# Other groups for 256 rows of w2 on the DMA engines, and their first quarter issued ahead of x

## Chip, cores and metric

The kernel runs on one core of a Trainium2 chip. The metric is the time of one execution on the device in microseconds (us). The span in a profile page is some 1.8 us shorter than that time. A run is labelled slow here when its time is over 1.5% above the fastest run of the same kernel, and fast otherwise.

## The reference, cut to what matters

Two tokens (B = 2, one position each) go through a normalisation, then through attention over the last 2048 positions of a cache, and beside it through a perceptron with a squared ReLU. All tensors are bf16.

```python
x = A_x                                   # [2, 1, 576]
xn = _layernorm(x)
return x + _A_ref(xn, A_k_cache, A_v_cache, A_wq, A_wo) + _B_ref(xn, B_w1, B_b1, B_w2, B_b2)

# _A_ref: 32 query heads, 16 heads of k and v, window W = 2048, head size 128
#   softmax(q k / sqrt(128)) v @ wo
# _B_ref:
h = jnp.einsum("bsd,df->bsf", x, w1) + b1          # F = 4608
h = jnp.where(h > 0, h, 0) ** 2                    # (shortened)
out = jnp.einsum("bsf,fd->bsd", h, w2) + b2        # w2 is [4608, 576]
```

Nearly all the time goes by while 53.6 MB of cache and weights are read. TensorE is busy for 70% of the span beside it, but the chain of work that ended last is 92% DMA (table below).

## The kernel before

Almost everything is loaded from the sync queue in large transfers over all 16 DMA engines. The last fourth of w2 has 1152 rows: 896 of them (FT = 7 rows for each of 128 partitions) come last of all on the sync queue, and 256 are taken out of that and loaded early from the scalar queue, in parts that only some of the engines carry. Every engine has the same bytes on the sync queue, so the grouping of these 256 rows decides, together with the instruction fetches, which engines end last.

`XS` holds the groups as (rows for a partition, partitions, engines): (3, 32, 8) is 96 rows on 32 partitions in four transfers of 8 partitions each, (8, 20, 5) is 160 rows on 20 partitions in four transfers of 5.

```python
    XS = ((3, 32, 8), (8, 20, 5))
    FT = (HW - sum(r * p for r, p, _ in XS)) // P      # 7
    # ... FX: first row of each group; CX: the columns of h that belong to the rows

    x_parts = [(s, i) for s, (_, xp, xe) in enumerate(XS) for i in range(xp // xe)]

    def issue_w2x():
        if x_parts:
            s, i = x_parts.pop(0)
            xr, xp, xe = XS[s]
            rows = B_w2[FX[s]:FX[s] + xr * xp, :].rearrange("(e i r) n -> i e (r n)", e=xe, r=xr)
            tc.keep_in_program_order(nc.scalar.dma_start(out=w2x_sb[s][i:xp:xp // xe, :], in_=rows[i]))

    xb_sb = const.tile([B + 1, D], BF16, name="xb_sb")
    x_sb = xb_sb[0:B, :]
    nc.scalar.dma_start(out=x_sb, in_=x2d)             # x: first on the scalar queue
    # ... sync queue: k of unit 0, wq; then the normalisation of x
```

The parts are issued one at a time, each after a load of k or v; the first after the load of v of unit 1. The matmuls that use them come late, when they have long landed.

```python
    def load_k(u):
        # ... sync queue
        if u >= 3:
            issue_w2x()

    def load_v(u):
        # ... sync queue
        if u >= 1:
            issue_w2x()

    def mlp_x():
        i = FT
        for w, (xr, xp, _) in zip(w2x_sb, XS):
            for r in range(xr):
                out_acc(mlp["h"][0:xp, N3 + i, :], lambda a, z: w[:, r * D + a:r * D + z])
                i += 1
```

## Time and profile before

| | before |
|---|---|
| time, median of 3 runs | 134.87 us (134.85 to 134.87) |
| span in the profile | 133.0 us |
| DMA share of the chain that ended last | 92% |
| rate of all 16 DMA engines in the middle | 430 GB/s |
| last weights land, on the span's clock | 129.66 us |

The table is read from the bottom: the last weights land at 129.66 us and only some 0.7 us of arithmetic follow. Between the start and that landing the DMA engines are full, so the time is made of bytes, of the rate at which they move, and of how evenly they are spread. The prediction shows the lines for this. First the rate in 40 equal slices of the span (GB/s, from the page): it stays near 430 from the second slice to the third from last.

```profile
GB/s 104 427 432 422 448 399 468 399 443 420 429 438 437 404 454 406 463 404 437 430 414 448 409 458 403 437 438 443 438 412 434 404 466 426 424 404 433 408 193 1
```

Then the start in order of time (start in us, duration, engine, line, what it does; ACTq is the scalar engine's sequencer, which issues the DMAs of the scalar queue):

```profile
0.72 0.56 ACTq L190 DMA_DIRECT2D xb_sb<-in_A_x_dram  x1
...
1.44 0.77 ACTq L186 DMA_DIRECT2D w2x_sb<-in_B_w_dram  x1
...
3.08 0.45 DVE L223 BATCH_NORM_STATS2 stats<-xb_sb 2x6 f32<-2x288 bf16 x1
...
6.62 0.51 PE L110 MATMUL pro_ps<-ident,tmp_x 2*128 2x2 bf16 x6 [6.62 <-DVE tmp_x L233]
```

The issue of x ends at 1.28 us, and its two packets start 0.4 us later, at 1.66 and 1.72. The first w2 part has been issued by 2.21, but its packets start at 5.70 to 5.94.

### The profile page before, as it was taken

The numbers are of one execution on the slowest core, as the hardware profiler recorded it, in microseconds if no ns is written. First come the engines' busy times: TensorE is split into PE (matmuls) and PEld (weight loads), VectorE is DVE, ScalarE is ACT, GpSimd is POOL, SyncE is SP. The second block draws the span as 40 slices with busy tenths as digits, with TensorE's granted clock in tenths as the row PEclk, the third lists the DMA queues.
The fourth block names the chain that finished last, engine by engine and source line by source line (L and its number), as shares of the span: only waits on it lengthen the run. The fifth ranks groups of instructions, "written<-read, shape, count | busy, mean of one in ns | idle before, by whom it ended". The sixth has DMA issues, their size and how long they took to land.

```text
span 133.0 us, 2082 instructions
## 1 busy us (share of the span) xinstructions
PE 93.0 (70%) x850; PEld 55.1 (41%) x850; DVE 58.8 (44%) x160; ACT 46.9 (35%) x65; POOL 5.4 (4%) x18
## 2 busy tenths in 40 slices
PE   0069646988597397767798597499785477829970
PEld 0059314465363243524554353437542144215640
DVE  6724405234575436457367684527430432070010
ACT  5715403177284263346385084343320400000010
POOL 7000000010100100010010100100010000000000
PEclk9999995559999959999999999657997775555698
DMA  3999999999999999999999999999999999999940
GB/s 104 427 432 422 448 399 468 399 443 420 429 438 437 404 454 406 463 404 437 430 414 448 409 458 403 437 438 443 438 412 434 404 466 426 424 404 433 408 193 1
DMA packets 4458, 53.74 MB, mean 404 GB/s; under 512 B 551, under 2 KB 682, under 8 KB 1230
## 3 DMA queue, kind: packets, MB, share of 16 engines
q1 hardware_dynamic: 4320, 53.32, 94.5%
q10 hardware_dynamic: 130, 0.31, 0.6%
q8 instruction: 6, 0.10, 0.3%
q14 instruction: 2, 0.02, 0.0%
HBM read 53.62 MB, written 0.00 MB: 403 GB/s over the span
## 4 chain that ended last, share of the span: by engine, by line
DMA 92%; PE 4%; SPq 1%; issue 0%; DVE 0%; DVEq 0%
DMA v<-in_A_v_cache_dram 43%; DMA k<-in_A_k_cache_dram 20%; DMA w<-in_B_w_dram 17%; DMA wq<-in_A_wq_dram 12%; PE kT_ps L110 2%; PE o_ps L107 1%; SPq L128 0%; SPq L135 0%; DVE fin_sb L594 0%; PE tail_ps L107 0%; DVEq L594 0%
## 5 line engine op out<-in xcount | busy, mean ns | idle before, releaser
L110 PE MATMUL kT_ps<-ident_f,k 128*128 128x128 f32 x256 | 42.8, 315 | 11.1 <-DMA k<-in_A_k_cache_dram 7.2
L110 PEld LDWEIGHTS kT_ps<-ident_f,k 128*128 128x128 f32 x256 | 33.3, 162 | 25.9 <-issue 11.4
L327 ACT COPY kT<-kT_ps 128x1024 bf16<-128x1024 bf16 x32 | 31.8, 1013 | 22.9 <-PE kT_ps L110 22.1
L329 DVE COPY kT<-kT_ps 128x1024 bf16<-128x1024 bf16 x32 | 21.9, 684 | 16.7 <-PE kT_ps L110 16.3
L107 PE MATMUL sc_ps<-kT,qz 128*32 128x512 bf16 x128 | 10.5, 413 | 5.8 <-DVE kT L329 5.8
L107 PE MATMUL o_ps<-v,pT 128*32 128x512 bf16 x128 | 12.1, 475 | 0.0
L359 ACT ACTIVATE p<-sc_ps,bias 128x512 bf16<-128x512 f32 x8 | 5.5, 687 | 17.9 <-DVE gown L355 17.9
L588 ACT COPY part<-out_ps 17x144 f32<-17x144 f32 x2 | 0.5, 268 | 23.8 <-DVE part L588 23.8
L348 DVE TENSOR_REDUCE m<-sc_ps 128x1 f32<-128x512 f32 x8 | 5.5, 692 | 7.2 <-PE sc_ps L107 7.2
L388 DVE SCALAR_TENSOR_TENSOR o<-o_ps,in_s,o 128x128 f32<-128x128 f32 x24 | 8.3, 346 | 0.5
L362 DVE STREAM_TRANSPOSE pT<-p 128x512 bf16<-128x512 bf16 x8 | 5.7, 710 | 6.4 <-ACT p L359 6.4
L386 DVE TENSOR_SCALAR o<-o_ps,in_s 128x128 f32<-128x128 f32 x8 | 2.7, 338 | 10.8 <-PE o_ps L107 10.8
L107 PE MATMUL out_ps<-wo,ws 128*17 128x288 bf16 x64 | 6.1, 364 | 1.6 <-DVE ws L421 1.6
L352 POOL PARTITION_ALL_REDUCE gmax<-m x8 | 2.9, 365 | 91.2 <-DVE m L350 91.2
L107 PEld LDWEIGHTS <-hT_sb 128*17 128x17 bf16 (+2 forms) x104 | 4.8, 105 | 4.0 <-issue 1.3
L107 PEld LDWEIGHTS <-qz 128*32 128x32 bf16 x128 | 2.2, 98 | 10.0 <-DVE kT L329 7.4
L107 PE MATMUL op_ps<-o,of_h 128*128 128x129 f32 x16 | 4.0, 339 | 3.3 <-DVE o L388 3.2
L107 PEld LDWEIGHTS <-xnT 128*2 128x2 bf16 x100 | 2.5, 94 | 8.6 <-issue 7.5
L107 PEld LDWEIGHTS <-ws 128*17 128x17 bf16 x64 | 3.5, 111 | 3.9 <-DVE ws L421 1.9
L110 PE MATMUL pro_ps<-ident,tmp_x 2*128 2x2 bf16 x6 | 0.5, 176 | 6.6 <-DVE tmp_x L233 6.6
L107 PEld LDWEIGHTS op_ps<-o,of_h 128*128 128x128 f32 x16 | 2.8, 221 | 5.3 <-DVE o L388 5.3
L107 PE MATMUL h_ps<-w,xnT 128*2 128x384 bf16 x48 | 3.2, 419 | 2.2 <-DMA w<-in_B_w_dram 2.2
(79 smaller groups left out, 58.5 us busy)
## 6 DMA issues: line engine op xcount, KB each, us to landing
k<-in_A_k_cache_dram SPq DMA_DIRECT2D x8, 2048.0 KB, 23.6
v<-in_A_v_cache_dram SPq DMA_DIRECT2D x8, 2048.0 KB
wo<-in_A_wo_dram SPq DMA_DIRECT2D x2, 2304.0 KB
w<-in_B_w_dram SPq DMA_DIRECT2D x2, 2304.0 KB
wq<-in_A_wq_dram SPq DMA_DIRECT2D x2, 2048.0 KB, 16.2
w<-in_B_w_dram SPq DMA_DIRECT2D x3, 1296.0 KB
w_rem<-in_B_w_dram SPq DMA_DIRECT2D x1, 576.0 KB, 35.2
w<-in_B_w_dram SPq DMA_DIRECT2D x1, 576.0 KB
```

What stands on the lines that cost most here:

```text
L107: tc.keep_in_program_order(nc.tensor.matmul(*a, **k))
L110: tc.keep_in_program_order(nc.tensor.transpose(*a, **k))
L327: nc.scalar.copy(out=kT, in_=kT_ps[:])
L329: nc.vector.tensor_copy(out=kT, in_=kT_ps[:])
L348: nc.vector.tensor_reduce(out=m1[:], in_=sc_ps[:], axis=AX.X, op=ALU.max)
L352: nc.gpsimd.partition_all_reduce(gmax[:], m2[:], channels=P, reduce_op=ReduceOp.max)
L359: nc.scalar.activation(out=p_sb[:], in_=sc_ps[:], func=ACT.Exp, bias=bias[:, 0:1], scale=scale, accum_out=o1[:, Dh:Dh + 1])
L362: nc.vector.transpose(out=pT[:].rearrange("p j r -> p (j r)"), in_=p_sb[:])
L386: nc.vector.tensor_scalar(scalar1=in_s[:, 0:1], scalar2=None, op0=ALU.mult, **kw)
L388: nc.vector.scalar_tensor_tensor(scalar=in_s[:, k:k + 1], in1=o1[:, 0:Dh], op0=ALU.mult, op1=ALU.add, **kw)
L588: cp(out=part[32 * i:32 * i + MB, :], in_=out_ps[32 * (i // 2):32 * (i // 2) + MB, (i % 2) * OQ:(i % 2 + 1) * OQ])
```

## The change

The intent: engines 0 to 4 end last because of their w2 rows, so 240 rows are spread over six engines (24 partitions of 10 rows, in four transfers of 6 partitions), and 16 over all engines (16 partitions of one row, one transfer). The first of the four transfers goes ahead of x, to lie in the stretch at the start in which the engines do nothing.

```diff
-    XS = ((3, 32, 8), (8, 20, 5))
+    XS = ((10, 24, 6), (1, 16, 16))
...
     xb_sb = const.tile([B + 1, D], BF16, name="xb_sb")
     x_sb = xb_sb[0:B, :]
+    issue_w2x()
     nc.scalar.dma_start(out=x_sb, in_=x2d)
```

## The prediction

> **What bounds the kernel now.** I read the page first (slices, queues, chain), then the busy time by stretches for the start and the end, then the chain of waits in order of time, and last the packet records and semaphore updates in the trace, which have a start, a duration, a size and a queue for each DMA packet.
>
> ```profile
> DMA  3999999999999999999999999999999999999940
> DMA packets 4458, 53.74 MB, mean 404 GB/s; under 512 B 551, under 2 KB 682, under 8 KB 1230
> q1 hardware_dynamic: 4320, 53.32, 94.5%
> q10 hardware_dynamic: 130, 0.31, 0.6%
> q8 instruction: 6, 0.10, 0.3%
> q14 instruction: 2, 0.02, 0.0%
> DMA 92%; PE 4%; SPq 1%; issue 0%; DVE 0%; DVEq 0%
> ```
>
> The transfers are busy from the first slice to the last but two and the chain that ended last is 92% DMA: what counts is when the last weights land. q1 is the sync queue (k, v and all weights), q10 the scalar queue (x, biases and the w2 rows of this change), q8 and q14 fetch instructions.
>
> Busy time by stretches, the last columns being granted clock, DMA share and GB/s:
>
> ```profile
> 0.00:1.60 1.60, 0.00 (x0) 0.00 (x0) 0.75 (x7) 0.28 (x1) 1.07 (x7) 1.00 0.00 0
> 1.60:2.10 0.50, 0.00 (x0) 0.00 (x0) 0.39 (x3) 0.50 (x1) 0.50 (x3) 1.00 0.02 5
> 60.00:120.00 60.00, 44.03 (x420) 24.88 (x418) 29.25 (x75) 19.46 (x27) 1.46 (x4) 0.82 1.01 430
> 126.60:127.20 0.60, 0.37 (x6) 0.14 (x3) 0.00 (x0) 0.00 (x0) 0.00 (x0) 1.00 0.84 338
> 127.20:128.10 0.90, 0.86 (x15) 0.72 (x16) 0.00 (x0) 0.00 (x0) 0.00 (x0) 1.00 0.69 270
> 128.10:128.70 0.60, 0.49 (x16) 0.18 (x14) 0.15 (x1) 0.00 (x0) 0.00 (x0) 1.00 0.42 154
> 128.70:129.40 0.70, 0.42 (x23) 0.27 (x25) 0.44 (x2) 0.14 (x1) 0.00 (x0) 1.00 0.10 36
> ```
>
> In the middle all 16 DMA engines are full (430 GB/s). At the end they stop one after another: between 126.6 and 129.4 us the idle shares weigh 0.6 x 0.16 + 0.9 x 0.31 + 0.6 x 0.58 + 0.7 x 0.90 = 1.35 us of every engine. The mean engine ends 1.35 us before the last one; so much an even load could give at most. At the start nothing moves for 1.6 us, and almost nothing until 2.1.
>
> The chain's last pieces (start, duration, what):
>
> ```profile
> 107.61 22.06 DMA w<-in_B_w_dram
> 129.66 0.04 issue
> 129.70 0.27 PE tail_ps L107 x4
> 129.97 0.03 DVEq L594
> 130.05 0.31 DVE fin_sb L594
> ```
>
> After the last w2 chunk lands (129.66) only 0.7 us of computing remain. TensorE waits for DMA little: in the timeline it idles 0.27 us at 127.24, about 0.1 at 128.6 and 0.28 at 129.32, with 0.04 before the last four matmuls. These 0.69 us are a second ceiling: were the weights earlier by more, TensorE would set the end.
>
> **Who is the last engine.** The packet records have no engine number, but on a full engine each packet starts where the one before ended (16384 B every 607 ns), and each engine runs the same 270 packets of q1 in the same order. That is enough to thread all packets into 16 tracks, and their scalar-queue packets tell which engines they are. When each track started its last semaphore packet (the landing follows 0.31 us later):
> - five tracks with 50.7 KB of w2 rows (engines 0 to 4): 128.59, 128.64, 128.64, and two that also carry a q14 instruction fetch, 129.17 and 129.35. These two have the 2304 B packet of the bias b1, so they are among engines 0 to 3;
> - three with 13.8 KB (engines 5 to 7): 127.26, and 128.63 and 128.68 with one q8 fetch each;
> - eight with none (8 to 15): four bare at 126.58 to 126.96, four with a q8 fetch at 128.13 to 128.20.
> A q8 fetch of 16 KB costs its engine 1.41 us (fetch and the stretched data packet after it take 2.02 us, less 0.607), the q14 fetches 0.76 and 0.58 us (129.35 and 129.17 less 128.59).
>
> **What the Trainium skill says.** "DMA: Bandwidth & Descriptors", Why a DMA increments its semaphore by 16 and not by 1: k is the largest number up to 16 that divides the slowest dimension of both sides, and on the hardware queues the lowest-numbered k engines are used, so 8, 5 and 6 rows go to engines 0-7, 0-4 and 0-5. The trace agrees for 8 and 5: eight tracks have the 3456 B packets and five of them the 9216 B ones. Same page, Queues, rings and completion order: each engine round-robins between rings packet by packet[...]; agrees, as q10 packets stand singly between q1 packets, and the last chunk's sixteen increments spread over 126.87 to 129.66 us. "Runtime: NRT & Kernel Launch", Instruction fetch mechanics: instructions come in 16 KiB blocks of 256; q8 shows six packets of 16384 B at 27.5, 49.1, 66.1, 83.4, 100.4 and 116.1 us, one per some 250 recorded TensorE instructions. TensorE's program is the same after the change, so I expect the same fetches. In order of time they hit two of engines 5 to 7, then four of 8 to 15; if they step up by one engine (inferred, not shown), that is 6 to 11, and engine 5 is the one without.
>
> **The change part by part.** Bytes and arithmetic stay: 256 rows before (3 x 32 + 8 x 20) and after (10 x 24 + 16), 11 stationary columns and 22 matmuls, the same FT = 7. The rows move.
> 1. Engines 0 to 4 lose four packets of 3456 and four of 9216 B. In the records each takes 131.5 and 343.5 ns to the next start, and its semaphore packet 5.5: 4 x 137 + 4 x 349 = 1944 ns.
> 2. Engines 0 to 5 get four packets of 11520 B. From 343.5 ns at 9216 and 385.5 at 10368: 427.5 + 5.5, times 4 = 1732 ns.
> 3. All 16 get one 1152 B packet: 47 + 5.5, some 53 ns.
> 4. Engines 6 and 7 lose 548 ns; engine 5 gains 1732 - 548.
> Sums: the worst two 129.35 and 129.17 - 1.944 + 1.732 + 0.053 = 129.20 and 129.01; the other three 128.43 to 128.48; engine 5 127.26 + 1.237 = 128.50; engines 6 and 7 128.14 and 128.18; the rest 0.05 later, at most 128.26. The worst gains 0.16 us by the regrouping alone.
> 5. The first quarter goes ahead of x. Today x, issued at 0.72 us, has its first packets at 1.66 and 1.72, and k's first packets start at 2.13 to 2.38. A 427 ns packet that starts at 1.7 on each of six engines lies in that empty stretch nearly whole; the later engines, some 60 ns apart like x's two, run into k's start by 0.1 or 0.2 us. But k's first packets take 0.88 to 1.39 us instead of 0.61 anyhow, so part of that may vanish too. I count 0.35 to 0.43 us off engines 0 to 5, 0.40 for the bounding ones.
> New last engine: 129.20 - 0.40 = 128.80, against 129.35: -0.55 us. That is under the 0.69 us that TensorE allows, so all of it reaches the end: 134.87 - 0.55 = 134.3; I put 134.35.
> What lies beside: x is issued some 0.7 us later and lands behind a large packet, perhaps at 3.5 us. The square root of the norm waits today for table loads until 5.63 us, which shift by the same 0.7; the first TensorE transposes of x go from 6.62 to 7.3 us and still end before k lands at 8.36. The scalar engine's instructions come in another order in the first three steps (the exponential stands after two copies instead of before). Loads are issued 20 us and more before they land, so such a shift doesn't starve the queue.
>
> **Rivals.** (a) The early packet is not hidden: k's packets start later on six engines. Then only 0.16 us is left, 134.7. For it: the two queues are issued at the same time and the sync issue already takes 0.63 us beside x's against 0.54 alone. Against it: the empty stretch.
> (b) A fetch lies on another engine than I think, or moves, as the scalar engine has fewer instructions. If engine 5 has a q8 fetch, it ends at 128.65 + 1.24 - 0.40 = 129.5 and the kernel is 0.15 us slower, 135.0. If a q14 fetch left engines 0 to 5, the worst were some 128.6 or 128.3; TensorE then caps the gain at 0.69, 134.2.
> (c) TensorE, at a granted clock of 0.55 between 120 and 126 us, ends the kernel by a slightly longer chain: the gain shrinks to some 0.3, 134.55.
> (d) The later x delays the query projection and so the first scores: with 20 us of queued loads it changes nothing at the end.
>
> **Range and chances.** From -0.16 (a) to -0.69 (ceiling), with room for a slower start and for (b): 133.95 to 134.85 holds eight in ten. All of it is far inside 2% (2.7 us): even an ideal load gives 1.35 us, 1%. Faster by over 2% 0.005, slower 0.01, within 0.985.
>
> **What would show it.** DMA share in the stretch before 2.1 us rising from nearly 0 to some 0.3; the last landing near 129.1 instead of 129.66 on the span's clock; the spread of the last sixteen increments shrinking from 2.8 to about 2.2 us; q8 still six packets and q14 two; TensorE's waits at the end nearly gone. Wrong if the landing moves by under 0.2 us (start not hidden), if the spread grows (fetch on engine 5), or if TensorE has no wait left while the end hasn't moved.

## The result, and the profile after

| | before | after |
|---|---|---|
| all runs of the same rounds, us | 134.85, 134.87, 134.87, 134.88 | 135.15, 134.79, 139.73, 140.47 |
| median | 134.87 | 137.44 |
| last weights land (profiled run, 135.15 us) | 129.66 | 130.02 |

The median of the changed kernel is 1.9% above that of the kernel before. Ratios in this document are the mean time of one kernel's fast runs over that of the other's fast runs of the same rounds, so they are not quite the ratio of the medians. Here the ratio is 1.0008, with a 95% interval from 0.9984 to 1.0032: it covers only the two fast runs of the changed kernel, on either side of the kernel before.

The two runs near 140 us carry the label slow. The kernel before ran 57 times, in turn with the other kernels and on the same chips, and was always between 134.76 and 135.09 us. Later profiles show the same loss in runs that are labelled fast, such as 136.97 us. So there are two questions: why is a good run not faster, and what makes a run bad?

**A good run.** The profiled run took 135.15 us. From its page, the scalar queue (q10, 0.31 MB as before) and the chain's shares; q8 and q14 again have six and two packets, the same lines as in the prediction:

```profile
q10 hardware_dynamic: 106, 0.31, 0.6%
...
DMA 85%; PE 10%; ACTq 1%; DVE 1%; issue 0%; DVEq 0%; ACT 0%
```

The start, in order of time, to be held against the same lines of before:

```profile
0.72 1.41 ACTq L186 DMA_DIRECT2D w2x_sb<-in_B_w_dram  x1
...
2.17 0.30 ACTq L191 DMA_DIRECT2D xb_sb<-in_A_x_dram  x1
...
7.74 0.81 DVE L224 BATCH_NORM_STATS2 stats<-xb_sb 2x6 f32<-2x288 bf16 x2 [3.19 <-DMA xb_sb<-in_A_x_dram]
...
9.80 0.51 PE L110 MATMUL pro_ps<-ident,tmp_x 2*128 2x2 bf16 x6 [9.80 <-DVE tmp_x L234]
```

The issue of the early part takes 1.41 us, so x is issued 1.45 us later than before (2.17 for 0.72) and lands at 7.71 us, not at 3.5; TensorE's transposes of x wait for it until 9.80. Nothing moved in the empty stretch (columns: stretch, us, then busy time and count of PE, PEld, DVE, ACT and POOL, granted clock, DMA share, GB/s; the other lines are the end of the kernel):

```profile
1.60:2.10 0.50, 0.00 (x0) 0.00 (x0) 0.40 (x3) 0.00 (x0) 0.50 (x3) 1.00 0.00 0
127.20:128.10 0.90, 0.51 (x10) 0.43 (x11) 0.00 (x0) 0.00 (x0) 0.00 (x0) 1.00 0.68 264
128.10:128.70 0.60, 0.60 (x14) 0.39 (x8) 0.00 (x0) 0.00 (x0) 0.00 (x0) 1.00 0.34 125
128.70:129.40 0.70, 0.59 (x20) 0.29 (x17) 0.49 (x2) 0.00 (x0) 0.00 (x0) 1.00 0.14 53
129.40:130.00 0.60, 0.30 (x8) 0.15 (x8) 0.11 (x1) 0.37 (x2) 0.00 (x0) 1.00 0.03 10
```

From 1.6 to 2.1 us the DMA share is 0.00, where I had predicted about 0.3. The packet records say when the early packets started: six of 11520 B at 5.00 to 5.05 us, in the midst of k. At the end the engines stop earlier than before in the mean (share 0.34 for 0.42 from 128.1 to 128.7 us), yet in the last line a share of 0.03 is left: less than one engine of 16 still works, and everything waits for it. Its landing closes the chain:

```profile
2.17 5.55 DMA xb_sb<-in_A_x_dram
...
107.94 22.08 DMA w<-in_B_w_dram
130.02 0.04 issue
130.07 0.26 PE tail_ps L107 x4
...
130.41 0.31 DVE fin_sb L595
```

The landing is 0.36 us later than before (130.02 for 129.66). Threading the packet records into one track for each engine, as in the prediction, gives the starts of the last semaphore packets:

| track | before | after |
|---|---|---|
| two of engines 0 to 3, with a q14 fetch | 129.17, 129.35 | 129.05, 129.23 |
| engines 0 to 3, without | 128.59, 128.64 | 128.27, 128.40 |
| engine 4 | 128.64 | 128.21 |
| engine 5 | 127.26 to 128.68 (one of the three of 5 to 7) | **129.67**, with a q8 fetch at 27.7 us |
| 6 and 7 | the other two of those | bare 126.37 to 127.04, |
| 8 to 15 | bare 126.58 to 126.96, with a fetch to 128.20 | with a fetch to 128.34 |

The last engine is one that was never last before. It has the large w2 packets but not the packet of b1, so it is engine 4 or 5; the experiments tell why I call it 5.

**A bad run** was not profiled in this round, so no trace shows the runs of 139.73 and 140.47 us themselves. The first experiment, the same kernel again, caught one.

### The profile page after: what moved, and what is told of

It reads as the page before. It is cut to its first block, busy times and chain, and to the rows that moved or that the text cites. A ratio compares the mean times of both kernels' runs of the same rounds, so it can differ in the third digit from the quotient of the medians.

```text
span 133.4 us, 2081 instructions
## 1 busy us (share of the span) xinstructions
PE 88.6 (66%) x850; PEld 52.0 (39%) x850; DVE 58.4 (44%) x160; ACT 46.6 (35%) x65; POOL 5.4 (4%) x18
## 4 chain that ended last, share of the span: by engine, by line
DMA 85%; PE 10%; ACTq 1%; DVE 1%; issue 0%; DVEq 0%; ACT 0%
DMA k<-in_A_k_cache_dram 32%; DMA v<-in_A_v_cache_dram 28%; DMA w<-in_B_w_dram 17%; PE kT_ps L110 7%; DMA w2x_sb<-in_B_w_dram 4%; DMA xb_sb<-in_A_x_dram 4%; PE o_ps L107 3%; ACTq L186 1%; PE sc_ps L107 1%; DVE stats L224 1%; DVE fin_sb L595 0%; PE tail_ps L107 0%; PE op_ps L107 0%; DVE mv L226 0%; DVEq L595 0%
## 5 line engine op out<-in xcount | busy, mean ns | idle before, releaser
L110 PE MATMUL kT_ps<-ident_f,k 128*128 128x128 f32 x256 | 40.4, 304 | 11.4 <-DMA k<-in_A_k_cache_dram 8.6
L110 PEld LDWEIGHTS kT_ps<-ident_f,k 128*128 128x128 f32 x256 | 31.2, 155 | 26.2 <-issue 14.5
L107 PE MATMUL sc_ps<-kT,qz 128*32 128x512 bf16 x128 | 9.7, 383 | 6.4 <-DVE kT L330 5.0
L107 PE MATMUL o_ps<-v,pT 128*32 128x512 bf16 x128 | 13.3, 519 | 0.0
L107 PE MATMUL out_ps<-wo,ws 128*17 128x288 bf16 x64 | 5.6, 341 | 1.6 <-DVE ws L422 1.6
```

Source lines behind the costliest of these rows:

```text
L107: tc.keep_in_program_order(nc.tensor.matmul(*a, **k))
L110: tc.keep_in_program_order(nc.tensor.transpose(*a, **k))
```

## The experiments

Sixteen kernels ran, in five groups (1 to 4, 5 to 8, 9 to 12, 13 to 15, and 16), on chips 7, 4, 7, 11 and 13; kernels of one group share their runs of the kernel before. Differences within a group are the safest, as the chip is the same. The theories: the runs near 140 us are a slow state of the chip or the launch and not of the kernel (called A where an expectation has letters); the late x delays what follows (B). Later there was a third: engines 0 to 5 lag behind the others and that stops something (S). Each fell, as told below.

### 1. The changed kernel again

No edit. It ran to see whether long runs come back on another occasion, and to catch one in a profile.

> The changed kernel once more, to see how often it falls to the long time and, with luck, to get a trace of it. Theory A (the long runs are a fault of the chip that day): all runs 134.8 to 135.2. Theory B (the long runs belong to the kernel: x now stands behind a large scalar-queue packet, and how long the pair waits behind k on the DMA engines differs from run to run): again two groups, near 135.0 and near 140, with a third to two thirds of the runs long.

Measured: 139.98, 136.44, 138.52, 139.40, 135.20, 136.78 us, beside eleven runs of the kernel before at 134.79 to 134.99. The run of 139.98 us is the profiled one. Its rate in 40 slices:

```profile
GB/s 147 405 436 420 426 439 432 413 441 425 432 424 383 379 360 370 370 360 375 356 379 368 436 427 427 446 426 427 427 427 434 425 436 426 428 419 426 412 166 1
```

Ten slices in the middle move 356 to 383 GB/s, all others but the ends about 430. By stretches (columns as above), ahead of it, in it and after it:

```profile
30.00:40.00 10.00, 5.12 (x36) 3.06 (x34) 3.79 (x8) 3.58 (x6) 0.37 (x1) 0.68 1.02 434
42.00:73.00 31.00, 24.24 (x195) 14.15 (x194) 15.65 (x38) 13.61 (x18) 1.09 (x3) 0.83 1.01 368
76.00:86.00 10.00, 6.37 (x51) 3.36 (x50) 5.37 (x14) 3.54 (x6) 0.37 (x1) 0.83 1.01 433
```

The DMA share is 1.01 in all three: the engines have work without a pause, and each packet takes longer. In the records a 16384 B packet takes 611 ns outside and about 720 inside, on all 16 engines alike. The good run of the changed kernel has no such stretch:

```profile
42.00:73.00 31.00, 25.07 (x227) 15.33 (x226) 18.61 (x45) 15.07 (x19) 1.09 (x3) 0.94 1.01 429
```

nor has the kernel before:

```profile
42.00:73.00 31.00, 23.15 (x201) 13.25 (x201) 17.56 (x43) 14.63 (x19) 1.09 (x3) 0.94 1.01 430
```

The size fits. In 31 us at 368 GB/s there is 31 x (1 - 368/430) = 4.5 us of lost transfer, and this run is 4.8 us above the good one (139.98 less 135.20). The stretch runs from about 41.4 to 74 us. At 41.1 to 41.9 us the records show the packets of the 16-row transfer, one for each engine. The kernel before sends nothing like it from the scalar queue. That made it the first suspect.

### 2. The new groups alone, x first

```diff
-    XS = ((3, 32, 8), (8, 20, 5))
+    XS = ((10, 24, 6), (1, 16, 16))
```

> The new groups (10 rows on 24 partitions, 1 on 16) with x issued first as before. Theory B: x lands near 2 us again, no long runs at all, all runs within 0.3 us of each other. Theory F (an instruction fetch of 16 KB lies on engine 5, which now carries 47 KB): the last track ends near 129.6 to 129.9 and the time is 134.9 to 135.4, slower than before by 0.1 to 0.5. If the prediction's reading was right (engine 5 free of fetches): 134.7.

Measured: 136.97, 136.22, 135.94, 136.76, 135.25, 136.71 us, all labelled fast, ratio 1.0106 [1.0074, 1.0139]. So the long runs come without the early issue: theory B falls as their cause. The trace of the 136.97 us run has a stretch from 53 to 64.6 us:

```profile
42.00:52.00 10.00, 8.31 (x84) 4.98 (x82) 5.75 (x14) 5.50 (x7) 0.36 (x1) 1.00 1.01 431
54.00:64.00 10.00, 7.47 (x75) 4.35 (x75) 5.84 (x14) 4.72 (x6) 0.37 (x1) 1.00 1.01 362
```

Here the 16-row packets lie at 51.7 to 53.1 us, as the kernel issues them one load of k or v later. The stretch has moved with them. The loss, some 11 us x (1 - 362/431) = 1.8 us, is most of the 2.1 us by which the run lies above the kernel before; the rest is the lagging engine.

### 3. The early issue alone, old groups

```diff
+    issue_w2x()
     nc.scalar.dma_start(out=x_sb, in_=x2d)
```

> The old groups with the first part (3 rows each on engines 0 to 7) issued ahead of x. Theory B: long runs near 140 appear here too, though nothing of the grouping changed; in short runs x lands 4 us later than before and the end is where it was, 134.7 to 135.0. If the long runs come from the grouping: none here.

Measured: 134.82, 134.76, 134.80, 134.82, 134.75 us, ratio 0.9993 [0.9982, 1.0005]. No run is long. In the trace the start is as in the changed kernel:

```profile
0.72 1.38 ACTq L186 DMA_DIRECT2D w2x_sb<-in_B_w_dram  x1
```

The issue takes 1.38 us, the early packets (3456 B here) start at 4.79 to 5.13 us and x's at 6.20 and 6.47. So x lands as late as in the changed kernel and costs nothing at the end: rival (d) of the prediction is right. The run can't tell whether the early packet is worth its full 0.13 us on eight engines, because the interval holds both that and nothing; the packet times say that it isn't hidden.

### 4. Two parts ahead of x

The changed kernel with `issue_w2x()` twice ahead of the load of x.

> The changed kernel with two quarters ahead of x instead of one. Theory B: x lands later still (over 9 us in the good case) and the long runs get more frequent or the only ones, 138 to 142; that would also give a trace of the long state. Theory A: 134.8 to 135.4.

Measured: 135.16, 135.38, 135.31, 135.74 us, ratio 1.0044 [1.0030, 1.0059]. The packets of the second part start at 6.57 to 6.75 us, right after the first's, and x's at 8.34 and 8.48. Doubling the early bytes hides nothing more and only delays x by another 1.7 us. The profiled run (135.16 us) has no slow stretch, though its 16-row transfer went at 31.5 to 33.2 us: that transfer doesn't always bring one. Nor did it in the good run of the result, where it went at 41.4 to 42.1 us.

### 5. The 16 rows on eight engines

```diff
-    XS = ((3, 32, 8), (8, 20, 5))
+    XS = ((10, 24, 6), (1, 16, 8))
```

With x first. The 16 rows now go in two transfers of 8.

> New groups of ten rows with x first, but the last 16 rows in two transfers on engines 0 to 7 instead of one on all 16. In the two long traces all 16 engines slow from 611 to 720 or 733 ns per 16 KB packet at once, 1 us after the 16-engine transfer, and stay slow for 12 to 33 us. Theory R (the transfer of one row on each of 16 engines sets this off): no slow stretch here, 134.7 to 135.3 by the fetch on engine 5. Theory S (the lag of engines 0 to 5 against the others sets it off): slow stretches remain, 135.3 to 140.

Measured: 135.06, 136.71, 135.47, 135.13, 135.10, 135.70 us, ratio 1.0049 [1.0018, 1.0081]. Far fewer long runs, but 136.71 is one, and only the 135.06 us run was traced. It is clean, and its last engine starts its last semaphore packet at 129.67 us, as in the changed kernel. What lengthened 136.71 stays open.

### 6. The 16-row transfer first of the parts

The kernel of experiment 2 with the last part moved to the front.

```diff
+    x_parts = x_parts[-1:] + x_parts[:-1]
```

> New groups with x first and the 16-engine transfer as the first w2 part, the four ten-row parts after it. Theory R: the slow stretch begins right after that transfer, near 7 us, or, if it needs more than that transfer, does not occur at all. Theory S: it begins after the last ten-row part, near 50 us, as in the trace with the old order, 135.3 to 140.

Measured: 136.30, 135.36, 135.28, 137.05, 136.87, 135.60 us, ratio 1.0090 [1.0051, 1.0129]. In the trace (136.30 us) the 16 packets go at 5.0 to 5.5 us and the stretch lies from 6 to 17:

```profile
6.00:17.00 11.00, 8.11 (x54) 6.51 (x55) 4.24 (x10) 4.05 (x4) 0.00 (x0) 1.00 1.02 395
20.00:30.00 10.00, 8.82 (x62) 4.75 (x55) 3.60 (x10) 2.60 (x6) 0.36 (x1) 0.55 1.01 432
```

At 5 us no engine has had a w2 row yet, so engines 0 to 5 cannot lag: theory S falls. Three kernels have now put the transfer at three times, and the stretch began within about 1 us of it each time.

### 7. The kernel before with one 16-row transfer added

All else is as before; after the last w2 part a dummy transfer of 16 rows of w2 goes to a tile that nothing reads.

```diff
-    const.tile([P, 96], F32, name="pad_0")
+    junk = const.tile([16, D], BF16, name="junk")
+    junk_done = []
...
+        elif not junk_done:
+            junk_done.append(1)
+            tc.keep_in_program_order(nc.scalar.dma_start(out=junk[:], in_=B_w2[FX[0]:FX[0] + 16, :]))
```

> The kernel before with one more transfer after its last w2 part: 16 rows of w2 into a scratch tile, one on each of the 16 engines, 53 ns each. Theory R: slow stretches start near 65 us, after this transfer, and runs spread over 135 to 138. Theory S: none, 134.9 to 135.0.

Measured: 139.93, 134.88, 143.45, 137.19, 140.84, 135.02 us. The two good runs equal the kernel before (ratio of fast runs 1.0006 [0.9989, 1.0024]); the others lose up to 8.6 us. In the trace of 139.93 us the 16 packets go at 71.0 to 71.7 us and the stretch lasts from 73 to 121 (ahead of it, its first part and its last):

```profile
60.00:70.00 10.00, 7.50 (x73) 4.44 (x70) 4.62 (x11) 5.19 (x7) 0.36 (x1) 1.00 1.01 429
74.00:84.00 10.00, 7.13 (x71) 4.22 (x67) 5.84 (x15) 4.72 (x6) 0.36 (x1) 1.00 1.02 391
...
114.00:121.00 7.00, 5.36 (x40) 2.30 (x40) 1.42 (x5) 0.00 (x0) 0.00 (x0) 0.50 1.00 384
```

This settles theory A: a kernel that was never long in 57 runs becomes long in four of six by 18 KB that nobody uses. The slow stretch belongs to that transfer.

### 8. 96 rows on all engines in place of 16

A layout that should do the balancing better: 160 rows on five engines as before, 96 rows over all 16.

```diff
-    XS = ((3, 32, 8), (8, 20, 5))
+    XS = ((8, 20, 5), (1, 96, 96))
```

> 160 rows in four parts of 8 rows on engines 0 to 4 and 96 rows in one transfer of six rows on every engine; engine 5 gets no more than its share. From the tracks of the kernel before: the worst engine ends at 129.35 - 1.94 + 1.40 + 0.29 = 129.10, so 134.6 if no slow stretch comes. Theory R: slow stretches after the transfer on 16 engines, 135 to 138. Theory S: none, since engines 0 to 4 lag less than before.

Measured: 135.78, 135.82, 136.04, 135.74, 135.85 us, ratio 1.0074 [1.0061, 1.0087]; a miss by 1.2 us, and steady. The transfer's packets, six for each engine, start from 50.2 to 54.6 us, and the trace is slow meanwhile: 395 GB/s from 50 to 54 us, with 16 KB packets up to 10% longer. That is 4 x (1 - 395/430) = 0.3 us, too little for 1.2 us, and where the rest goes I did not find out.

### 9. The added transfer, spread over the partitions

Experiment 7 with the destination on every eighth partition, 0 to 120.

```diff
+            tc.keep_in_program_order(nc.scalar.dma_start(out=junk[0:P:8, :], in_=B_w2[FX[0]:FX[0] + 16, :]))
```

> The kernel before with the same extra 16-row transfer, but its rows written to partitions 0, 8, 16 and so on to 120 instead of 0 to 15. Theory D (sixteen engines meet while they write into the same few partitions): no slow stretch, all runs 134.9 to 135.0. Theory Q (it is that all 16 engines turn aside to a second queue at nearly the same time): slow stretches as with partitions 0 to 15, some of the six runs at 137 to 143.

Measured: 134.94, 135.01, 135.02, 134.97, 135.22 us, ratio 1.0013 [1.0001, 1.0025]. No run is long, and the trace is clean where that of experiment 7 was slow:

```profile
74.00:84.00 10.00, 8.78 (x61) 5.53 (x58) 4.98 (x12) 3.92 (x6) 0.37 (x1) 0.66 1.01 431
```

### 10. The added transfer, its rows from far apart

Experiment 7 with the destination as there (partitions 0 to 15) and 16 rows spread over the whole of w2.

```diff
+            tc.keep_in_program_order(nc.scalar.dma_start(out=junk[:], in_=B_w2[0:F:F // 16, :]))
```

> The same, written to partitions 0 to 15, but its rows read from all over w2 (every 288th row) instead of 18 KB in a row. Theory M (sixteen engines meet on one short piece of memory): no slow stretch, all 134.9 to 135.0. Theories D and Q: some runs at 137 to 143.

Measured: 136.71, 134.95, 136.90, 142.92, 143.48, 135.04 us. As bad as experiment 7; the trace of 136.71 us has the stretch from 74 us on, with the transfer at 72.7 to 73.5:

```profile
74.00:85.00 11.00, 7.74 (x76) 4.34 (x75) 7.44 (x18) 4.74 (x7) 0.36 (x1) 1.00 1.01 375
```

It is the side that is written that matters, not where the rows are read. Experiment 9 ran in the same rounds on the same chip, so the two compare without a change of chip.

### 11. Eight rows added in place of 16

```diff
+            tc.keep_in_program_order(nc.scalar.dma_start(out=junk[0:8, :], in_=B_w2[FX[0]:FX[0] + 8, :]))
```

> The same with 8 rows on engines 0 to 7 instead of 16 on all. Theory Q: no or rare slow stretches, as the kernel before has four such transfers and never ran long in 40 runs. If some runs are long: it is the lateness of the transfer, not its sixteen engines.

Measured: 135.08, 135.05, 134.99, 134.96, 134.98 us, ratio 1.0010 [0.9997, 1.0023]; no long run, and the trace is clean. The scratch tile stands in place of a padding tile, so the tiles behind it may lie elsewhere; here and in 12 this is as in 7 and 10, so it is not what makes runs long.

### 12. The added transfer on the sync queue

Experiment 7 with `nc.sync` in place of `nc.scalar`.

> The same 16 rows issued on the sync queue between two tiles of the caches, so that no engine has to turn to another queue. Theory Q: none slow, 134.9 to 135.0. Theories D and M: some runs at 137 to 143.

Measured: 135.03, 134.93, 134.93, 134.89, 134.89 us, ratio 1.0005 [0.9993, 1.0017]; no long run, and the trace is clean:

```profile
74.00:84.00 10.00, 7.16 (x74) 4.22 (x67) 6.35 (x16) 4.62 (x6) 0.36 (x1) 1.00 1.02 436
```

The same 16 rows to the same partitions do no harm in the queue that carries all the rest. One thing changed along with the queue: the sixteen packets now start over 2.9 us (76.88 to 79.78), where in the five traces with a long stretch they started within 0.5 to 1.4 us. So the queue and the packets' coming together are not told apart. Coming together is not enough by itself: in experiment 9 they came within 0.8 us.

### 13. The changed kernel, its 16 rows on the sync queue

```diff
-            tc.keep_in_program_order(nc.scalar.dma_start(out=w2x_sb[s][i:xp:xp // xe, :], in_=rows[i]))
+            queue = nc.sync if xe > 8 else nc.scalar
+            tc.keep_in_program_order(queue.dma_start(out=w2x_sb[s][i:xp:xp // xe, :], in_=rows[i]))
```

> The changed kernel with its last part, 16 rows on 16 engines, issued on the sync queue; all else the same. If that transfer on the scalar queue is the cause of the long runs: none over 135.6, and two values, near 134.8 and near 135.2, by whether an instruction fetch falls on engine 5. If not: again a third to two thirds of the runs at 136 to 140.

Measured: 135.20, 135.24, 135.35, 135.31, 134.81, 135.12 us, ratio 1.0019 [1.0007, 1.0031]. The long runs are gone, and the stretch that was slow in experiment 1 is full:

```profile
42.00:73.00 31.00, 25.61 (x226) 15.41 (x226) 18.81 (x45) 14.97 (x19) 1.10 (x3) 0.93 1.01 430
```

What is left is the good run's loss: the trace again has one lagging engine, whose last semaphore packet starts at 129.72 us.

### 14. The new groups, x first, the 16 rows on the sync queue

The kernel of experiment 2 with the same queue line.

> The new groups with x first as before and the 16 rows on the sync queue. If the transfer is the cause: 134.7 to 135.3, no slow stretch, where the same kernel with the scalar queue gave 135.25 to 136.97. Against the kernel above it shows what the early issue is worth: by the tracks nothing, within 0.1 us.

Measured: 135.23, 135.09, 134.72, 134.69, 135.01, 134.87 us, ratio 1.0002 [0.9991, 1.0014]. No run is long. The traced one is the 135.23 us run, with its lagging engine at 129.77 us. The runs lie between two ends, 134.7 and 135.2. The median is 134.94 for 135.22 in experiment 13, more than the 0.1 us that was expected; six runs of each, with both ends in both, can't say whether that is the early issue or how often a fetch falls on the lagging engine. Neither kernel had a long partner on this chip: that the queue is the cure rests on 12 beside 10 for one chip, and on 13 and 14 across chips.

### 15. Two short-row transfers over all engines, on the sync queue

A further try at a better balance; the copies after the transposes of h are written as a loop over the groups.

```diff
-    XS = ((3, 32, 8), (8, 20, 5))
+    XS = ((4, 20, 5), (1, 80, 80), (1, 96, 96))
...
+            queue = nc.sync if xe > 8 else nc.scalar
```

> A balance that avoids both faults: x first, 80 rows in four parts of 4 on engines 0 to 4, and 176 rows as 80 and 96 partitions, 5 and 6 rows on every engine, on the sync queue; six stationary columns instead of eleven. From the tracks of the kernel before: the worst engine 129.35 - 1.94 + 0.72 + 0.53 = 128.66, one of 8 to 15 with a fetch 128.20 + 0.53 = 128.73; so 0.62 us less than before, 134.2. If small packets or a slow stretch eat it: 134.9 and more.

Measured: 136.32, 136.27, 136.30, 136.39 us, ratio 1.0105 [1.0092, 1.0118]: a miss by 2.1 us. The short rows go at about 58 and 63.7 us, and there the rate falls:

```profile
58.00:64.00 6.00, 5.22 (x47) 3.09 (x49) 3.10 (x7) 3.04 (x3) 0.00 (x0) 0.90 1.02 388
```

That window holds 6 x (1 - 388/430) = 0.6 us of the 2.1; the rest was not traced to a cause.

### 16. 96 rows on 32 partitions over all engines, on the sync queue

```diff
-    XS = ((3, 32, 8), (8, 20, 5))
+    XS = ((8, 20, 5), (3, 32, 32))
...
+            queue = nc.sync if xe > 8 else nc.scalar
```

> 160 rows in four parts of 8 on engines 0 to 4 as in the kernel before, and the other 96 as 3 rows on each of 32 partitions, two packets of 3456 bytes per engine, in one transfer on the sync queue; x first. From the tracks of the kernel before: the worst engine 129.35 - 1.94 + 1.40 + 0.27 = 129.08, those with a fetch at most 128.5, so 0.27 us less than before whatever engine a fetch falls on: 134.6, all runs within 0.2 us. If the short packets on all engines set off a slow stretch here too: 135 to 137.

Measured: 135.38, 135.11, 135.24, 135.31, 135.45 us, ratio 1.0034 [1.0020, 1.0047]; a miss by 0.7 us, with a short slow stretch as well:

```profile
57.00:61.00 4.00, 3.09 (x33) 1.91 (x25) 2.80 (x8) 3.14 (x5) 0.20 (x1) 1.00 1.03 376
```

Its cost is some 4 x (1 - 376/430) = 0.5 us. The two last experiments bound the finding of 12 to 14: the sync queue is free of the long stretch for the 16-row transfer, but larger transfers of short rows over all engines cost more there than their bytes. No kernel beats both of the two compared.

### What the runs say together

| runs | count | over 135.6 us |
|---|---|---|
| kernel before | 57 | 0 |
| 16 rows to partitions 0 to 15, from the scalar queue, over 16 engines (the changed kernel, 1, 2, 4, 6, 7, 10) | 38 | 24 |
| no such transfer, or spread, or of 8 rows, or on the sync queue (3, 5, 9, 11 to 14) | 38 | 2 (both of 5) |

Experiments 8, 15 and 16, with larger transfers of short rows, are not in the table: they are slower in every run, and their losses are explained only in part.

The long stretch was traced only where three properties met: 16 engines (7 and 10 against 11), the destination in partitions 0 to 15 (7 and 10 against 9), and the scalar queue (7 and 10 against 12). On one chip, in the same rounds, 10 was long in four of six runs and 9, 11 and 12 in none of fifteen. The untraced 136.71 us of experiment 5, without such a transfer, stays an exception, and with the queue the spacing of the packets changed too (12). What happens in the chip is not shown. The Trainium skill, "DMA: Bandwidth & Descriptors", section Back-pressure in remote DMA, says that a saturated port on the written side holds up the engines behind it and their other queues. It says so of transfers between cores; that the destination decides here (9 against 10) would fit such a cause within one core, but no run shows a port. Why the state lasts for 11 to 48 us after packets of 50 ns, and why it ends, is open. In several traces it ends near an instruction fetch (74.1 us in experiment 1, 121.1 in 7, 64.6 in 2); I saw this and did not test it. It is no rule: the fetches at 51.2 us in experiment 1 and at 84.4 and 102.7 in 7 ended nothing, and in experiment 6 the stretch ended near 17.6 us with no fetch there.

**Which engine lags.** Of the fifteen traces that I threaded, seven are of kernels with the old groups: there engines 0 to 4 never had a q8 fetch, and engines 5 to 7 had two or none. In all eight traces with the new groups exactly one of engines 4 and 5 had one. The one that can have a fetch in the old groups is engine 5, so I take it to be that; the records don't number engines, so this is inferred. Which of the six fetches hits it changes from launch to launch, even for the same kernel: the first (at 27.7 us) in the profiled run of the result, the third (74.1 us) in experiment 1. All eight traced runs with the new groups had such a fetch, and clean ones among them took 135.06 to 135.23 us. The runs at 134.7 to 134.8 us (134.79 of the result, 134.72 and 134.69 of 14) fit launches without one on engine 5; none of them was traced.

## Why the prediction was wrong

The prediction was 134.35 us, within 133.95 to 134.85; the median is 137.44, and of the first four runs only 134.79 lies in the range. That it stays within 2% by the median (1.9%) is luck: half of the first four runs are over 3.5% longer.

**Steps 1 to 3, the sums for engines 0 to 3: right.** Without the hidden part the prediction put the two tracks with a q14 fetch at 129.20 and 129.01 us; they are at 129.23 and 129.05. So the worth of a packet by its size holds within 0.04 us, and the gain of 0.16 us by regrouping was there on these engines (0.12 measured). The other engines of this class are at 128.21 to 128.40, for 128.43 to 128.48.

**Step 3, "some 53 ns" for the 16-row transfer: the failed step behind the median.** The packets do take 51 ns. The step counted their bytes and nothing beyond. What they set off costs 1.8 us in experiment 2, 4.5 in experiment 1 (this kernel), and 8.6 by time in the worst run of 7. Neither the profile of before nor any rival had a sign of it: before has no transfer of this kind.

**Step 4, engine 5 "is the one without" a fetch: failed.** I took the order of the fetches over the engines for a rule that goes on ("if they step up by one engine"), from a single trace. The placement changes from launch to launch. Rival (b), engine 5 with a fetch, is what happened in the good runs. Its size was nearly right: without the hidden 0.40 it puts engine 5 at 129.9 us, and the track is at 129.67, which is 1.46 us after engine 4's 128.21. Its 135.0 us is close to the 135.15 of the profiled run.

**Step 5, 0.40 us hidden at the start: failed, it was 0.** I read the empty stretch from 0 to 2.1 us as room for any transfer issued first. x's two packets did use it, but a part over six engines was issued in 1.41 us, beside the issues of the sync queue, and its packets started only at 5.0, behind k. The hint was in the trace of before: its first w2 part was issued by 2.21 us and its packets came at 5.7. Going first moved them to 5.0, from 5.54 in experiment 2, and not to 1.7. Rival (a) had this.

**Rivals (c) and (d).** TensorE did not set the end: it waits 0.89 us at 127.59 and 0.30 at 129.70 in the good run. x was to be issued 0.7 us later and was issued 1.45 later, as the early part took 1.41 us to issue; it landed 4 us later than I thought and still costs nothing (experiment 3). "Loads are issued 20 us and more before they land" was too broad: wq lands 16.2 us after its issue, and the first k, issued at 0.72, at 8.36.

Of the signs that the prediction named, three said wrong: no DMA share ahead of 2.1 us, the last landing later by 0.36 us and not earlier, and the last sixteen increments spread over 3.3 us (126.73 to 130.02), not 2.2.

## What to carry to other kernels

Balance DMA engines by their packet records, and leave about one fetch (1.4 us here) of slack on each engine that may get an instruction fetch, because the next launch may place it elsewhere; no kernel here shows a gain from such slack (8 and 16 tried it and were slower). An idle stretch at the start is room only for what can start in it: look when the packets of such a transfer have started before, not when it was issued. Treat a small transfer over all engines into a few partitions, from a second queue, as a suspect, and run a change several times before you believe a profile of one good run.

## What the Trainium skill lacked or had wrong

- "DMA: Bandwidth & Descriptors" has nothing of a state in which all 16 engines slow down together within one core: 611 ns for a 16 KB packet become about 680 to 730, 430 GB/s become 362 to 395, for 11 to 48 us, set off by a transfer of 16 rows from the scalar queue into partitions 0 to 15, and not by 8 rows, by 16 on the sync queue or by 16 spread over the partitions. Its Back-pressure section speaks of transfers between cores only.
- "Runtime: NRT & Kernel Launch", Instruction fetch mechanics, calls the cost of crossing a 16 KiB block mostly hidden. Whether the engine that executes waits was not looked at; the DMA engine that carries the fetch loses 1.41 us, and in a kernel bound by DMA this sets the end (the engine taken to be 5, at 129.67 us). It doesn't say that the DMA engine differs from launch to launch of the same kernel, as here (first fetch in one, third in another).
- "DMA: Bandwidth & Descriptors", Queues, rings and completion order, describes engines that take turns between queues packet by packet. The packets here do stand singly between those of the sync queue, but those of a part that the scalar queue had issued by 2.13 us started at 5.0, almost 3 us later; the page has no such wait.
- The same page, Issuing engines are not separate DMA queues, says that issuing from several engines saves issue time only, which is usually small beside the transfer. At the start, beside the issues of the sync queue, one scalar issue took 1.41 us, where it takes about 0.7 later in the same kernel.
